# W' = w3·w_out in plain float32 matmuls, from decoded weights that are not split

## Chip, core and metric

One core of one Trainium2 chip runs the kernel. The time is device microseconds (us) of one execution. The kernel shown here took 947.56 us (median of 3 runs, 945.53 to 948.35).

## What is computed

The inputs come as float64, and the kernel decodes each weight to float32 itself. An attention of 4 batches and 8 heads (a pooled one and a local band) gives x of 2304 tokens by 512. Then, cut to what matters:

```python
a = x @ w1                      # 2304 x 1024
b = x @ w2
h = a * b @ w3                  # w3: 1024 x 1024
x = h @ w_out                   # w_out: 1024 x 512
h = x @ w_in                    # 2304 x 2048
out = (h * sigmoid(h)) @ w_out2 # 2304 x 512
```

The kernel multiplies w3 and w_out first, into W' (1024 x 512), so that the two products of the third and fourth line become one, `(a * b) @ W'`. The change is in how W' is made.

## The kernel before

**Weights.** A piece of a weight is 128 x 512 numbers of 8 bytes. `load_w` (L110) issues its DMA on SP's queue into a staging tile `st`; there are four of them in the opening, so up to four pieces are under way. `decode` makes float32 of it: one ScalarE instruction (ACT, L123) takes the high word's magnitude, and four VectorE instructions (DVE, L133, L137, L142, L147) shift and join the bits, in a tile `dec`. The last of the four is the last to read `st`, and frees it for the next load. `parts` then splits the float32 number in two: ACT rounds it to fp32r, the high part (`nc.scalar.copy`, L159), and DVE subtracts to get the low part (L160). A split weight is a tile of two layers, `[P, 2, 1024]`.

**Products.** Matmuls of split operands are made in three passes (`PASSES`): high by high, low by high, high by low. `wprime(i)` (L407) is a quarter of the work on one pair of tiles: two column blocks j, each with three matmuls of 128 x 512 into a PSUM tile `wp`; four quarters use up one w3 tile. In all it issues 192 matmuls from 8 w3 tiles (named `w_w` in the trace; two buffers) and 4 w_out tiles (`w_wA`; four buffers). Finished sums are split into `w_wC` (L421, L422).

**Order.** The opening is laid out by `events`: 36 attention steps (`run_steps`), 32 quarters of `wprime`, and decoding jobs with due slots. The jobs are 8 pieces of w_out, 16 of w3 and the first 8 of w1 and w2 (`w_wB`). The tile scheduler takes that list and fixes one order for each engine; within an engine instructions run strictly in that order. SP's queue too is in order: loads of the attention's q, k and v (`qk`, `vw`, `vr`) stand between the weight loads. The attention's matmuls are plain float32: scores `sd`, `s`; outputs `od`, `ol`; transposes `td`, `tl`. After the opening the a and b products (`ab`, L500), the product with W' (`y`, L533) and the second network (`h`, L670 and `o`, L697) follow; w1 and w2's last 8 pieces are decoded during the first `ab` products.

Of the kernel before, what the change touches and what calls it, by code (L numbers as in the profile page):

```python
# [8 lines left out]
F32 = mybir.dt.float32  # L9
# [5 lines left out]
NB, NHP, S, P = 4, 4, 576, 128  # L15
# [10 lines left out]
PASSES = ((0, 0), (1, 0), (0, 1))  # L26
I32 = mybir.dt.int32
# [5 lines left out]
def tile_model(ctx: ExitStack, tc: tile.TileContext, qk, vw, vr, w12, w3t, wo, wb, out):  # L33
    nc = tc.nc
    wide = wo.dtype != F32
# [20 lines left out]
    def mm_tile(name):  # L56
        return ps.tile([P, 512], F32, tag="mm", name=name, bufs=4)
# [27 lines left out]
    W = {}  # L85
    raw = {}
    homes = [stg]
    dec_homes = [stg, w3pool]
# [15 lines left out]
    def load_w(key, t):  # L104
# [8 lines left out]
            nc.sync.dma_start(st, src)  # L113
        raw[key, t] = (st, home)

    def decode(pair):

        todo = []
        for key, t, where, tag, bufs in pair:
            st, home = raw.pop((key, t))  # L120
            if wide:
                v = dec_homes[t % len(dec_homes)].tile([P, 512], I32, tag="dec", name="dec", bufs=2)
                nc.scalar.activation(v.bitcast(F32), st[:, :, 1].bitcast(F32), AF.Abs)  # L123
                todo.append((v, st))
            else:
                todo.append((st, st))

        def bits():
            if not wide:
                return  # L130
            for v, st in todo:
                f = v.bitcast(F32)
                nc.vector.tensor_scalar(  # L133
                    out=f, in0=f, scalar1=E_LOW, scalar2=E_HIGH, op0=ALU.max, op1=ALU.min
                )
            for v, st in todo:
                nc.vector.tensor_scalar(  # L137
                    out=v, in0=v, scalar1=3, scalar2=0x3FFFFFF8,
                    op0=ALU.logical_shift_left, op1=ALU.bitwise_and,
                )  # L140
            for v, st in todo:
                nc.vector.scalar_tensor_tensor(  # L142
                    out=v, in0=st[:, :, 1], scalar=-0x40000000, in1=v,
                    op0=ALU.bitwise_and, op1=ALU.bitwise_or,
                )
            for v, st in todo:
                nc.vector.scalar_tensor_tensor(  # L147
                    out=v, in0=st[:, :, 0], scalar=29, in1=v,
                    op0=ALU.logical_shift_right, op1=ALU.bitwise_or,
                )  # L150

        def parts():
            for (key, t, where, tag, bufs), (v, st) in zip(pair, todo):
                if t == 0:
                    W[key] = where.tile([P, 2, 1024], F32R, tag=tag, name="w_" + tag, bufs=bufs)
                f = v.bitcast(F32) if wide else v
                hi = W[key][:, 0, t * 512:(t + 1) * 512]
                lo = W[key][:, 1, t * 512:(t + 1) * 512]
                nc.scalar.copy(hi, f)  # L159
                nc.vector.tensor_tensor(out=lo, in0=f, in1=hi.bitcast(F32), op=ALU.subtract)  # L160

        bits()
        parts()

    def key_pieces(key, where, tag, bufs=None):
# [230 lines left out]
    def wprime(i):  # L396
        step, q = divmod(i, 4)
        half, gp = divmod(step, 4)
        k, jj = divmod(q, 2)
        w3v = W["w3", (gp, half)].rearrange("p l (k f) -> p l k f", k=2)  # L400
        wov = W["wo", gp].rearrange("p l (k e) -> p l k e", k=2)
        for j in (2 * jj, 2 * jj + 1):
            if gp == 0 and k == 0:
                wp_ps[j] = mm_tile(f"wp{half}_{j}")
            acc = wp_ps[j]
            for n, (a, b) in enumerate(PASSES):
                nc.tensor.matmul(  # L407
                    acc, lhsT=w3v[:, a, k, j * P:(j + 1) * P], rhs=wov[:, b, k, :],
                    start=(gp == 0 and k == 0 and n == 0),
                    stop=(gp == 3 and k == 1 and n == 2),  # L410
                )
        if q == 3:
            W.pop(("w3", (gp, half)))
        if gp == 3 and k == 1:
            for j in (2 * jj, 2 * jj + 1):
                m = 4 * half + j
                acc = wp_ps[j]
                if m % 2 == 0:
                    WP[m // 2] = wpool.tile([P, 2, 2, 512], F32R, tag="wC", name="w_wC")
                d = WP[m // 2]  # L420
                nc.scalar.copy(d[:, 0, m % 2, :], acc)  # L421
                nc.vector.tensor_tensor(  # L422
                    out=d[:, 1, m % 2, :], in0=acc, in1=d[:, 0, m % 2, :].bitcast(F32),
                    op=ALU.subtract,
                )
# [18 lines left out]
    for n, slot in enumerate((0, 1, 3, 5, 7, 8, 10, 11)):  # L444
        m, t = 4 + n // 2, n % 2
# [10 lines left out]
    def run_plan(slot):  # L456
        while n_jobs[0] < len(jobs) and jobs[n_jobs[0]][0] <= slot:
            pieces = jobs[n_jobs[0]][1]
            n_jobs[0] += 1
            n_done[0] += len(pieces)  # L460
            decode(pieces)
            load_to(n_done[0] + 4)
# [12 lines left out]
    for when, kind, i in sorted(events):  # L475
        if kind == 0:
            run_plan(when)
        elif kind == 1:
            wprime(i)
        else:  # L480
            run_steps(i + 1)
# [135 lines left out]
    def wb_next():  # L617
        n = n_split[0]
        if n >= min(32, 2 * len(wb_home)):
            return  # L620
        where, tag, bufs = wb_home[n // 2]
        wb_load(n + 1)
        decode([(("wb", n // 2), n % 2, where, tag, bufs)])
        n_split[0] += 1
        wb_load(n + 1 + 2 * len(homes))
# [88 lines left out]
    for s in range(16 * NT + LAG):  # L714
        if s < 16 * NT:
            t, f = divmod(s, 16)
# [65 lines left out]
```

## Time and profile before

| What | Value |
|---|---|
| Median of 3 runs | 947.56 us |
| The profiled execution's own time | 947.99 us |
| Its span in the profile | 946.2 us |
| PE busy | 892.4 us (94%) |
| DVE busy | 459.7 us (49%) |
| ACT busy | 317.1 us (34%) |
| Chain that ended last: PE, DVE, DMA, ACT | 73%, 12%, 6%, 4% |

PE is TensorE, PEld its weight loads, POOL is GpSimd. Busy shares are means over the whole run. The kernel has stages with different limits, so the table alone does not say what bounds the stage of the change. PEclk is the granted share of TensorE's clock: 1.00 is 2.4 GHz, 0.50 is 1.2 GHz, and a value between is a mean over time at both.

### The profile page before, as it was taken

Reading aid. Unit: us, or ns where it says so; the run is one execution under the profiler, and the core shown is the slowest. Engines: PE = TensorE matmul, PEld = TensorE weight load, DVE = VectorE, ACT = ScalarE, POOL = GpSimd, SP = SyncE. Lnnn points to the kernel's source line nnn. Section 1 sums busy time; section 2 is a strip of 40 time slices with the busy share of each in tenths; the row PEclk is TensorE's granted clock in tenths of the full one; section 3 lists DMA queues with packets and bytes.
Section 4 is the critical chain, followed back from the end, with each engine's and each line's share of the span. In section 5 each row is a group of like instructions: output and inputs, shape, how many; then the busy total and the mean of one; then the engine's idle time right before and its main releaser. Section 6 shows DMA issues by size and latency. Waiting matters only on the chain.

```text
span 946.2 us, 15978 instructions
## 1 busy us (share of the span) xinstructions
PE 892.4 (94%) x6224; PEld 802.3 (85%) x6224; DVE 459.7 (49%) x997; ACT 317.1 (34%) x966; POOL 258.0 (27%) x269
## 2 busy tenths in 40 slices
PE   5767789999999999999999998999999999999998
PEld 4545578899989999999999897989989989999897
DVE  7888999635453444324637999222221221222221
ACT  6466675443333333334224533211211211111111
POOL 1000014434243333324112154422422423322221
PEclk9787999999999999999999999999999999999999
DMA  8555544221422121121512544200200000000000
GB/s 272 167 179 182 185 132 127 63 76 56 139 78 77 58 72 53 31 68 40 178 65 75 185 139 133 63 6 1 68 1 1 34 1 1 34 1 1 35 1 34
DMA packets 26285, 73.58 MB, mean 78 GB/s; under 512 B 2912, under 2 KB 10080, under 8 KB 26208
## 3 DMA queue, kind: packets, MB, share of 16 engines
q1 hardware_dynamic: 26208, 72.54, 24.3%
q8 instruction: 49, 0.80, 0.4%
q14 instruction: 28, 0.23, 0.1%
HBM read 63.09 MB, written 9.44 MB: 77 GB/s over the span
## 4 chain that ended last, share of the span: by engine, by line
PE 73%; DVE 12%; DMA 6%; ACT 4%; issue 3%; POOL 1%; SPq 0%; DVEq 0%; ACTq 0%; POOLq 0%
PE o L697 19%; PE h L670 19%; PE ab L500 18%; PE y L533 9%; DVE dec L142 3%; DMA st<-wb 3%; DVE dec L147 2%; DMA st<-w3t 2%; PE ol L341 1%; PE s L300 1%; DVE dec L133 1%; DMA st<-w 1%; DVE dec L137 1%; PE tl L325 1%; ACT dec L123 1%
## 5 line engine op out<-in xcount | busy, mean ns | idle before, releaser
L681 POOL TENSOR_TENSOR g<-gf,g 128x384 fp32r<-128x384 f32 x96 | 104.8, 1092 | 275.9 <-DVE g L680 275.9
L678 DVE TENSOR_TENSOR gf<-h,sg 128x384 f32<-128x384 f32 x96 | 53.4, 556 | 258.7 <-ACT sg L676 258.7
L676 ACT ACTIVATE sg<-h 128x384 f32<-128x384 f32 x96 | 47.0, 491 | 290.3 <-PE h L670 290.3
L500 PE MATMUL ab<-x,w_wA 128*128 128x320 f32 (+1 forms) x768 | 112.7, 300 | 0.8 <-DVE w_wA L160 0.8
L500 PE MATMUL ab<-x,w_wB 128*128 128x320 f32 (+1 forms) x768 | 113.2, 300 | 0.0
L533 PE MATMUL y<-c,w_wC 128*128 128x320 f32 (+1 forms) x768 | 111.2, 299 | 0.0
L500 PEld LDWEIGHTS ab<-x,w_wA 128*128 128x128 f32 x768 | 103.2, 188 | 4.4 <-issue 2.0
L500 PEld LDWEIGHTS ab<-x,w_wB 128*128 128x128 f32 x768 | 103.6, 188 | 2.6 <-issue 0.8
L533 PEld LDWEIGHTS y<-c,w_wC 128*128 128x128 f32 x768 | 102.9, 188 | 2.7 <-issue 1.6
L518 POOL TENSOR_TENSOR c<-cf,c 128x320 fp32r<-128x320 f32 (+1 forms) x64 | 54.8, 856 | 140.2 <-DVE c L517 120.5
L407 PE MATMUL wp<-w_wA,w_w 128*128 128x512 f32 x192 | 63.4, 477 | 13.1 <-ACT w_w L159 12.0
L123 ACT ACTIVATE dec<-st 128x512 f32<-128x512 f32 x72 | 48.4, 674 | 69.9 <-DMA st<-wb 30.9
L224 ACT ACTIVATE E<-E,sm 128x70 f32<-128x70 f32 x144 | 49.0, 342 | 49.0 <-DVE sm L220 49.0
L407 PEld LDWEIGHTS wp<-w_wA,w_w 128*128 128x128 f32 x192 | 41.4, 228 | 24.9 <-ACT w_w L159 14.1
L514 DVE TENSOR_TENSOR cf<-ab,af 128x320 f32<-128x320 f32 (+1 forms) x64 | 29.0, 453 | 66.3 <-PE ab L500 60.1
L697 PE MATMUL o<-w_wA,g 128*128 128x512 f32 x216 | 55.7, 401 | 4.2 <-POOL g L681 3.6
L670 PE MATMUL h<-yhl,w_wC 128*128 128x384 f32 x288 | 55.2, 341 | 0.0
L670 PE MATMUL h<-yhl,w_wB 128*128 128x384 f32 x288 | 54.2, 337 | 0.5 <-ACT yo L542 0.5
L670 PE MATMUL h<-yhl,w_wA 128*128 128x384 f32 x288 | 54.4, 337 | 0.0
L697 PE MATMUL o<-w_wB,g 128*128 128x512 f32 x216 | 54.2, 395 | 0.0
L697 PE MATMUL o<-w_wC,g 128*128 128x512 f32 x216 | 54.1, 395 | 0.0
L670 PEld LDWEIGHTS h<-yhl,w_wC 128*128 128x128 f32 x288 | 52.0, 191 | 2.2
(92 smaller groups left out, 1377.6 us busy)
## 6 DMA issues: line engine op xcount, KB each, us to landing
st<-wb SPq DMA_DIRECT2D x32, 512.0 KB, 4.1
qk<-qk SPq DMA_DIRECT2D x16, 579.0 KB, 3.8
st<-w3t SPq DMA_DIRECT2D x16, 512.0 KB, 5.2
st<-w SPq DMA_DIRECT2D x16, 512.0 KB, 4.6
vw<-vw SPq DMA_DIRECT2D x16, 360.0 KB, 3.7
vr<-vr SPq DMA_DIRECT2D x16, 320.0 KB, 3.2
st<-ydram SPq DMA_DIRECT2D x12, 384.0 KB, 3.3
out<-os SPq DMA_DIRECT2D x18, 256.0 KB, 2.1
```

Source lines behind the costliest of these rows:

```text
L123: nc.scalar.activation(v.bitcast(F32), st[:, :, 1].bitcast(F32), AF.Abs)
L224: nc.scalar.activation(E[:, j, :], src[:, j, :], AF.Exp, bias=nb[:, j:j + 1], scale=scale, accum_out=sv[:, j:j + 1],)
L407: nc.tensor.matmul(acc, lhsT=w3v[:, a, k, j * P:(j + 1) * P], rhs=wov[:, b, k, :], start=(gp == 0 and k == 0 and n == 0), stop=(gp == 3 an ...
L500: nc.tensor.matmul(acc[:, :N], lhsT=wv[:, i, w, kk, :], rhs=x[:, j, :], start=(n == 0), stop=(n == 11),)
L514: nc.vector.tensor_tensor(out=cf, in0=acc[:, :N], in1=C.pop("af"), op=ALU.mult)
L518: nc.gpsimd.tensor_tensor(out=c[:, 1], in0=cf, in1=c[:, 0].bitcast(F32), op=ALU.subtract)
L533: nc.tensor.matmul(acc[:, :N], lhsT=WP[kf // 2][:, i, kf % 2, ec * P:(ec + 1) * P], rhs=c[:, j, :], start=(kf == 0 and n == 0), stop=(kf = ...
L670: nc.tensor.matmul(acc[:, :TT], lhsT=w[:, i, kk, :], rhs=y[:, j, kk, :], start=(n == 0), stop=(n == 11),)
L676: nc.scalar.activation(sg, acc[:, :TT], AF.Sigmoid)
L678: nc.vector.tensor_tensor(out=gf, in0=acc[:, :TT], in1=sg, op=ALU.mult)
L681: nc.gpsimd.tensor_tensor(out=g[:, 1], in0=gf, in1=g[:, 0].bitcast(F32), op=ALU.subtract)
L697: nc.tensor.matmul(acc_ps[t][j], lhsT=g[:, a, j * P:(j + 1) * P], rhs=w[:, b, 512:1024], start=(f == 0 and n == 0), stop=(f == 15 and n == 2),
```

## The change

Pieces of w3 and w_out are decoded straight into the tile from which the matmuls read, as float32, and are not split. `whole` gives that place: one `[P, 2, 512]` tile for two pieces of w3, and one `[P, 2, 2, 512]` tile for four pieces of w_out. `wprime` then makes one plain float32 matmul where three fp32r ones stood, 64 in all. w1, w2 and the second network's weights are decoded and split as before.

```diff
+    def whole(key, t, where, tag, bufs):
+        kind, i = key
+        if kind == "w3":
+            if t == 0:
+                W[key] = where.tile([P, 2, 512], I32, tag=tag, name="w_" + tag, bufs=bufs)
+            return W[key][:, t, :]
+        if i % 2 == 0 and t == 0:
+            W["wo2", i // 2] = where.tile([P, 2, 2, 512], I32, tag=tag, name="w_wo", bufs=bufs)
+        W[key] = W["wo2", i // 2][:, i % 2]
+        return W[key][:, t, :]
...
             st, home = raw.pop((key, t))
+            if key[0] in ("wo", "w3"):
+                v = whole(key, t, where, tag, bufs)
...
+            elif wide:
+                v = dec_homes[t % len(dec_homes)].tile([P, 512], I32, tag="dec", name="dec", bufs=2)
             if wide:
-                v = dec_homes[t % len(dec_homes)].tile([P, 512], I32, tag="dec", name="dec", bufs=2)
...
         def parts():
             for (key, t, where, tag, bufs), (v, st) in zip(pair, todo):
+                if key[0] in ("wo", "w3"):
+                    continue
...
-            for n, (a, b) in enumerate(PASSES):
-                nc.tensor.matmul(
-                    acc, lhsT=w3v[:, a, k, j * P:(j + 1) * P], rhs=wov[:, b, k, :],
-                    start=(gp == 0 and k == 0 and n == 0),
-                    stop=(gp == 3 and k == 1 and n == 2),
-                )
+            nc.tensor.matmul(
+                acc, lhsT=w3v[:, k, j * P:(j + 1) * P], rhs=wov[:, k, :],
+                start=(gp == 0 and k == 0), stop=(gp == 3 and k == 1),
+            )
```

The scheduler makes new orders from this. Line numbers of the changed kernel are 18 to 20 higher behind the new function (L123 is L141, L341 is L361, L407 is L426).

On PE, here is the first w3 tile's work in the kernel before, from the third column block of its first half on (`wp` are the W' sums, `w_w_185` the w3 tile, `tl`, `od`, `ol` the attention's):

```order
L407 MATMUL wp_2_326<-w_wA,w_w_185 128x512 x3
L407 MATMUL wp_3_330<-w_wA,w_w_185 128x512 x3
L325 MATMUL tl_0_0_300<-ident,E_0_152 70x128 x2
L325 MATMUL tl_0_2_304<-ident,E_0_152 70x128 x3
L407 MATMUL wp_0_311<-w_wA,w_w_185 128x512
L407 MATMUL wp_1_315<-w_wA,w_w_185 128x512
L285 MATMUL od_319<-EdT_192,vd_205 64x144 x4
```

And the same place in the changed kernel, where the w3 tile is `w_w_172` and the w_out tile `w_wo`:

```order
L426 MATMUL wp_2_297<-w_wo,w_w_172 128x512
L426 MATMUL wp_3_299<-w_wo,w_w_172 128x512
L345 MATMUL tl_0_0_275<-ident,E_0_152 70x128 x2
L345 MATMUL tl_0_2_279<-ident,E_0_152 70x128 x2
L426 MATMUL wp_0_286<-w_wo,w_w_172 128x512
L345 MATMUL tl_0_2_279<-ident,E_0_152 70x128
L305 MATMUL od_290<-EdT_186,vd_199 64x144 x4
```

Each three has become one, at nearly the same places among the attention's matmuls.

On SP's queue, these are the weight loads of the third group (w_out, then w3) and what stands around them, before:

```order
L110 DMA st<-w3t 128x1024 x2
L188 DMA vw_488<-vw 80x1152
L110 DMA st<-wo 128x1024 x2
L110 DMA st<-w3t 128x1024 x2
L181 DMA qk_587<-qk 128x1158
```

And in the changed kernel:

```order
L110 DMA st<-w3t 128x1024 x2
L110 DMA st<-wo 128x1024 x2
L208 DMA vw_427<-vw 80x1152
L110 DMA st<-w3t 128x1024 x2
L201 DMA qk_505<-qk 128x1158
```

The load of `vw` has moved behind the two w_out loads.

On ACT, the changed kernel has this around the decoding of the third w3 tile, `w_w_334` (what an instruction waits for stands in brackets; `DMAHW` is a load's landing):

```order
L256 ACTIVATE E_1_256<-E_1_256,sm 128x70 [waits Activation_49] x3
L141 ACTIVATE w_wo<-st 128x512 [waits DMAHW7_49]
L244 ACTIVATE Ed_356,sm<-sd_349,sm 128x144 [waits DVE_49,PE_49]
L141 ACTIVATE w_w_334<-st 128x512 [waits DMAHW0_49,PE_49]
L244 ACTIVATE Ed_356,sm<-sd_349,sm 128x144 x2
L346 COPY ET_1_371<-tl_1_0_372 70x256 [waits PE_49]
```

Before, a decode wrote `dec` first, and only the split wrote the w3 tile:

```order
L123 ACTIVATE dec<-st 128x512 [waits DMAHW6_49,DVE_49]
L159 CAST w_w_263<-dec 128x512 [waits DVE_49]
L123 ACTIVATE dec<-st 128x512 [waits DMAHW7_49,Activation_49]
L159 CAST w_w_263<-dec 128x512 [waits DVE_49]
L224 ACTIVATE E_1_281,sm<-E_1_281,sm 128x70 [waits DVE_49]
```

The casts are gone from ACT's order, and the first instruction of a decode now waits for PE as well, which must be done with the w3 tile whose buffer it writes.

## Rows read from the trace of the kernel before

**Rows 1.** Busy us (instructions) by stretch: PE, PEld, DVE, ACT, POOL; PEclk; DMA; GB/s.

```profile
0.00:134.50 134.50, 96.20 (x631) 69.94 (x632) 113.68 (x255) 83.90 (x256) 5.46 (x15) 0.86 0.60 191
134.50:175.00 40.50, 36.37 (x326) 32.69 (x325) 40.46 (x83) 23.00 (x77) 15.96 (x16) 1.00 0.33 101
175.00:580.00 405.00, 400.00 (x3488) 376.05 (x3486) 214.88 (x473) 153.40 (x527) 130.33 (x144) 1.00 0.29 89
580.00:946.00 366.00, 359.81 (x1786) 323.58 (x1784) 90.73 (x190) 56.77 (x109) 106.20 (x95) 1.00 0.06 21
```

**Rows 2.** Groups on DVE, 0 to 134.5 us: busy us, mean ns, idle before.

```profile
L160 DVE TENSOR_TENSOR w_w<-dec,w_w 128x512 fp32r<-128x512 f32 x16 | 10.7, 686 | 6.6 <-ACT w_w L159 6.6
...
L160 DVE TENSOR_TENSOR w_wA<-dec,w_wA 128x512 fp32r<-128x512 f32 x8 | 5.4, 682 | 0.0
```

**Rows 3.** Groups on ACT, 0 to 134.5 us, same columns.

```profile
L159 ACT CAST w_w<-dec 128x512 fp32r<-128x512 f32 x16 | 9.4, 611 | 4.9 <-DVE dec L147 4.9
...
L159 ACT CAST w_wA<-dec 128x512 fp32r<-128x512 f32 x8 | 4.9, 613 | 0.4 <-DVE dec L147 0.4
```

**Rows 4.** Chain that ended last, in the opening: start us, length us, what.

```profile
12.99 0.59 DVE w_wA L160
...
28.86 4.69 DMA st<-w3t
...
42.94 0.27 ACT w_w L159
...
61.77 3.78 PE wp L407 x8
...
91.64 0.60 DVE w_w L160
...
104.69 1.71 PE wp L407 x4
...
110.32 4.73 DMA st<-w
...
117.28 0.52 ACT w_w L159
...
117.84 2.08 PE wp L407 x4
```

**Rows 5.** Groups on PE, whole run: plain float32 scores and transposes.

```profile
L300 PE MATMUL s<-qk 64*64 64x70 f32 x576 | 27.8, 238 | 6.1 <-DVE E L310 3.1 <-ACT Ed L224 3.0
L325 PE MATMUL tl<-ident,E 128*70 128x128 f32 x144 | 25.2, 287 | 8.6 <-DVE ods L290 3.0 <-ACT EdT L275 2.4 <-ACT E L236 1.6
```

**Rows 6.** The chain where PE works without a pause, at PEclk 1.00.

```profile
186.75 0.88 PE sd L251 x12
...
201.75 0.55 PE tl L325 x5
...
589.80 2.10 PE o L697 x9
```

**Rows 7.** SP's queue in order of time, 36 to 52 us.

```profile
42.31 0.33 SPq L188 DMA_DIRECT2D vw<-vw  x1
42.74 0.84 SPq L110 DMA_DIRECT2D st<-wo  x2
```

**Rows 8.** DVE and ACT in order of time, 28 to 50 us.

```profile
33.62 0.68 ACT L123 ACTIVATE dec<-st 128x512 f32<-128x512 f32 x1 [1.65 <-DMA st<-w3t]
...
37.27 1.28 DVE L147 SCALAR_TENSOR_TENSOR dec<-st,dec 128x512 int32<-128x512 int32 x2
...
48.42 0.69 DVE L160 TENSOR_TENSOR w_w<-dec,w_w 128x512 fp32r<-128x512 f32 x1 [3.79 <-ACT w_w L159]
```

**Rows 9.** PE's W' matmuls in order of time: the ends of the first two w3 tiles.

```profile
22.82 2.36 PE L407 MATMUL wp<-w_wA,w_w 128*128 128x512 f32 x9
...
42.20 5.46 PE L407 MATMUL wp<-w_wA,w_w 128*128 128x512 f32 x22
```

**Rows 10.** The W' matmuls, 0 to 134.5 us: busy us, mean ns, idle before.

```profile
L407 PE MATMUL wp<-w_wA,w_w 128*128 128x512 f32 x192 | 63.4, 477 | 13.1 <-ACT w_w L159 12.0 <-DVE w_wC L422 0.8 <-DVE dec L133 0.3
```

More of the change, by code (lines that the diff above doesn't have):

```diff
@@ L120, in decode @@
             st, home = raw.pop((key, t))
+            if key[0] in ("wo", "w3"):
+                v = whole(key, t, where, tag, bufs)
+                if not wide:
+                    nc.vector.tensor_copy(v.bitcast(F32), st)
+                    continue
+            elif wide:
+                v = dec_homes[t % len(dec_homes)].tile([P, 512], I32, tag="dec", name="dec", bufs=2)
             if wide:
-                v = dec_homes[t % len(dec_homes)].tile([P, 512], I32, tag="dec", name="dec", bufs=2)
                 nc.scalar.activation(v.bitcast(F32), st[:, :, 1].bitcast(F32), AF.Abs)
@@ L153, in parts @@
             for (key, t, where, tag, bufs), (v, st) in zip(pair, todo):
+                if key[0] in ("wo", "w3"):
+                    continue
                 if t == 0:
@@ L399, in wprime @@
         k, jj = divmod(q, 2)
-        w3v = W["w3", (gp, half)].rearrange("p l (k f) -> p l k f", k=2)
-        wov = W["wo", gp].rearrange("p l (k e) -> p l k e", k=2)
+        w3v = W["w3", (gp, half)].bitcast(F32)
+        wov = W["wo", gp].bitcast(F32)
         for j in (2 * jj, 2 * jj + 1):
```

## Prediction

> **What bounds the kernel now.** I first read the busy times by stretch [rows 1]. From 175 us on PE is busy 400.0 of 405 and 359.8 of 366 us: whatever comes earlier moves the end by the same amount, as long as it only shifts this part. From 134.5 to 175 us DVE is busy 40.46 of 40.50 us, with work that the change leaves alone (the decoding of the last eight pieces), so this stretch is also shifted as a whole. The change therefore acts in the opening, 0 to 134.5 us, and pays what it takes from the opening's end. There no engine is full: DVE 113.7 us (85%), PE 96.2 us (72%, at a mean clock of 0.86), ACT 83.9 us.
>
> Since no engine fills the opening, busy time alone doesn't price the change. The second view is the chain that ended last [rows 4]: it runs mostly along DVE, and five times (the first at 28.86 us, the last at 110.32 us) leaves it for a weight load of some 5 us and ACT's start of a decode. The third, order of time on SP, DVE and ACT [rows 7, 8], shows why DVE stands idle at one place.
>
> **What is removed.** 24 pieces (16 of w3, 8 of w_out) lose the cast and the subtraction. On DVE that is 10.7 + 5.4 = 16.1 us [rows 2], on ACT 9.4 + 4.9 = 14.3 us [rows 3]. These are upper bounds of what each engine can give. What counts first is what of them stands on the chain [rows 4]: nine pieces of `w_w` or `w_wA` L160, the first of 0.59 us at 12.99 and the last of 0.60 us at 91.64, sum 5.59 us; and five pieces of L159, from 42.94 to 117.28 us, sum 2.84 us. The first of these, 0.27 us, lies in a stall that I count below, which leaves 2.57. Removed: 8.2 us. The rest of the 16.1 us lies beside loads, ACT and PE in the opening, and I count it at nothing; if that cover went with it, 16.1 us is the gain (first rival).
>
> **What is put in its place on PE.** 192 fp32r matmuls become 64 plain ones. Where PE works without pause, nine fp32r matmuls of 512 columns take 2.10 us [rows 6], 0.233 us each, so three take 0.700 us and all 44.8 us at the full clock. A plain 128x512 matmul is not in this trace; three kinds of plain float32 rows bound it. A plain matmul leaves two records: the program issues 18 score matmuls for each of 16 units, 288, and the trace has 576, while the 9 transposes per unit leave 144, one each [rows 5]. Five transposes of 128 columns take 0.55 us [rows 6], 0.110 us a record; four times the columns and two records make 0.880 us for a plain 128x512 matmul. Twelve records of `sd` with 144 columns take 0.88 us. They use quarters of the array, and if they ran one by one, 512 columns would cost 2 x 0.0733 x 512/144 = 0.52 us; if always two ran side by side, 1.04 us. I take the transposes' 0.880 us, since these fill the rows of the array as the new matmuls do; the ends are 0.52 and 1.04. That is 1.257 times the three that go (0.745 to 1.490), and 56.3 us in all: PE gets 11.5 us more work at the full clock.
>
> Three pieces of W' matmuls stand on the chain, 3.78 + 1.71 + 2.08 = 7.57 us [rows 4]. Times 1.257 they cost 1.9 us more (from 1.9 less to 3.7 more). The other W' matmuls are covered by PE's 38.3 us of idle time; that cover gone is the last rival.
>
> A rule to weigh against this price: the Trainium skill, FP8 and Floating Point Precision, TensorE Precision Notes, says that a true float32 product takes four passes through the array, where a reduced one reads the number once. Four passes at the 0.233 us of a row would be 0.93 us a matmul, and the term on the chain 2.5 us instead of 1.9; no row here shows a 512-column one, and the rule makes the change dearer by 0.6 us, not wrong.
>
> **What is moved.** In SP's order the load of `vw` stood ahead of two w_out loads, and now stands behind them. Before, it waited for PE and was issued at 42.31 us; the w_out loads came behind it at 42.74 us [rows 7], although the last readers of the first staging tile had started at 37.27 us and the two were done by 38.55 [rows 8]. DVE then stood idle for 3.79 us, since the cast that it needed was queued on ACT behind the start of a decode that waited for these loads. With the loads issued some 5 us earlier and the cast gone, I take the whole 3.8 us off. The next two loads, of w3, are now the first behind `vw`. They wait for the same step of PE, whose W' matmuls ahead of it are fewer but longer; I take no stall for them, because DVE has the two w_out pieces to decode meanwhile, four instructions each. If they do stall, the 3.8 us are lost again.
>
> **What is added: a wait.** The first ACT instruction of a w3 decode now writes the w3 tile, of which there are two, so it waits until PE has finished with the tile before last. Behind it in ACT's order stand softmax steps (`Ed`) and copies of `ET` from PSUM; DVE's four instructions of that piece wait for it, and PE for those. In the trace of before the first W' tile's matmuls were done at 25.2 us [rows 9], and the third w3 tile's first load was taken up at 33.62 us [rows 8]; the second tile's were done by 47.7 us at the latest [rows 9]. Loads come some 4 us earlier and PE is about 1.4 us later per tile (24 x 0.233 x 0.257), so the first of these waits is covered by the load's landing. I count all six at nothing; if each cost its 1.4 us, that would be 8.6 us. Less than nothing it can't be, since it only delays.
>
> **The sum,** against the profiled execution's 947.99 us (0.43 above the median of 947.56): -5.6 (DVE on the chain) -2.6 (ACT on the chain) +1.9 (PE on the chain) -3.8 (the stall behind `vw`) = -10.1, so **937.9 us**.
>
> **Rivals.**
> 1. *DVE was the true bound of the opening.* With every subtraction gone the end moves by all 16.1 us: 931.9 us. For it speaks that DVE is 85% busy in the opening and full behind it; against it, that the chain leaves DVE for loads five times. It needs the loads to keep ahead of a DVE that is faster by 0.68 us a piece.
> 2. *The stall only changes its place.* The w3 loads, now right behind `vw`, are late in the w_out loads' stead. Then only the chain's own pieces go: 947.99 - 6.3 = 941.7 us.
> 3. *The new wait is paid.* All six w3 tiles wait for PE, 8.6 us: 946.5 us, no change that can be told.
> 4. *PE becomes the bound of the opening* (slower). PE is idle for 38.3 us there, of which 12.0 us is W' waiting for the casts that go [rows 10]; 26.3 us of other waits would stay. PE's busy 96.2 us grow by 11.5/0.86 = 13.4 us at the mean clock, and by 23 us at half the clock: 135.9 to 145.5 us instead of 134.5, so 1.4 to 11 us slower, in the middle 954 us. It decides once the added work is over the 12.0 us that go. For it speaks that the attention's matmuls are queued among the W' ones, so that each longer one delays a softmax; against it, that a part of the 26.3 us is waiting for DVE, which now has less to do.
>
> On the last one the clock matters. PEclk is 0.86 in the opening and 1.00 in the stretches where PE is busier [rows 1]. The Trainium skill, TensorE: Matmul & The Clock Gate, Part 1, says that the slow clock is the default and that activity releases it. By that, a denser PE gets the full clock for longer and the added work nears 11.5 us, below the 12.0 that go. The trace's two stretches agree. I give the rival 12% and not more.
>
> **Chances and range.** Forecast (about 934 to 941) 42%, rival 1 20%, rival 2 17%, rival 3 9%, rival 4 12%. A measurement of this kernel tells a change from none at about 0.3%, 2.8 us: the forecast and rivals 1 and 2 are faster (79%), rival 3 the same (9%), rival 4 slower (12%). The range takes in rival 1 with a little room below and rival 3 above: 930.5 to 947.0. It leaves out rival 4 and some 4% at the low end. The bounds of the plain matmul's price (+1.8 and -3.8 us around the sum) lie inside.
>
> **What would show it.** In the profile after: no L159 and L160 for w3 and w_out, DVE's busy time less by about 16 us, ACT's by about 14. Plain W' matmuls in 128 records, following each other at about 0.44 us where PE doesn't pause (0.26 or 0.52 at the bounds). The first `ab` matmul about 10 us earlier than before, and all from there on shifted by as much, with the same lengths. The w_out loads of the third group issued close to the freeing of their tiles. It would be wrong if the start of a w3 decode on ACT waits for PE by microseconds (rival 3); if PE is busy nearly all of the opening (rival 4); if the w3 loads behind `vw` leave DVE idle (rival 2); or if DVE's idle time in the opening is as it was, so that the full 16 us come off (rival 1).

## The result, and the profile after

The changed kernel takes 930.39 us (median of 4 runs, 928.24 to 932.21), the kernel before 946.54 us (4 runs). The ratio is 0.983, 95% interval 0.9808 to 0.9852: about 16 us faster, a little under the low end of the range (930.5 to 947.0) and well over the 10.1 us of the sum. Rival 1, 931.9 us, has the number that came. One of the twelve executions of e2 below took 1711.85 us, and its ratio leaves that one out.

The busy times by stretch of the changed kernel (columns as in [rows 1]); the opening ends 16 us earlier, so the stretches start 16 us earlier too:

```profile
0.00:118.50 118.50, 95.66 (x578) 51.08 (x579) 99.92 (x236) 72.44 (x236) 5.47 (x15) 0.97 0.69 217
118.50:159.00 40.50, 36.69 (x335) 33.12 (x336) 39.28 (x82) 22.87 (x81) 17.65 (x18) 1.00 0.33 101
...
159.00:564.00 405.00, 399.45 (x3470) 375.31 (x3468) 213.41 (x468) 151.69 (x519) 128.81 (x142) 1.00 0.29 89
564.00:930.00 366.00, 359.99 (x1787) 323.72 (x1785) 91.53 (x190) 56.69 (x109) 106.09 (x95) 1.00 0.07 21
```

All behind the opening is as it was, within 1.8 us an engine and stretch, and from 159 us on PE is busy nearly all the time (399.45 of 405 us, then 359.99 of 366). In the opening PE is busy for nearly the same time in a shorter stretch, and its clock is at 0.97 instead of 0.86.

To compare the openings at the same point of the program, I take the stretch up to DVE's first instruction on an `ab` product (`cf`). First the kernel before, then the changed one:

```profile
0.00:139.70 139.70, 101.40 (x666) 74.98 (x667) 118.84 (x266) 87.34 (x268) 6.97 (x16) 0.87 0.58 186
```

```profile
0.00:121.00 121.00, 98.16 (x595) 53.58 (x596) 102.42 (x242) 74.38 (x243) 5.75 (x16) 0.97 0.68 215
```

DVE has 24 instructions fewer (266, 242) and 16.4 us less to do, and reaches the point 18.7 us earlier. Its idle time is 20.9 us before and 18.6 us after: the work taken off came off the time in full, with some idle time besides, and waits for loads, ACT and PE did not fill the hole.

Of those 18.7 us some were lost again at one place behind the opening, in this execution. PE's order of time there, in the changed kernel:

```profile
247.25 0.49 PE L288 MATMUL td<-ident,Ed 128*72 128x128 f32 x3
250.04 0.52 PE L288 MATMUL td<-ident,Ed 128*72 128x128 f32 x3 [2.30 <-DVE xf L372]
250.32 2.90 PE L518 MATMUL ab<-x,w_wA 128*128 128x320 f32 x12
```

And in the kernel before:

```profile
265.27 0.49 PE L268 MATMUL td<-ident,Ed 128*72 128x128 f32 x3
267.25 0.52 PE L268 MATMUL td<-ident,Ed 128*72 128x128 f32 x3 [1.49 <-DVE xf L352]
267.53 2.02 PE L500 MATMUL ab<-x,w_wA 128*128 128x320 f32 x12
```

Up to here the changed kernel is 18.0 us ahead (265.27 to 247.25). PE then waits 2.30 us instead of 1.49, and the twelve matmuls behind take 2.90 us instead of 2.02. What is left at the end is 946.2 - 930.4 = 15.8 us of span.

### The profile page after: what moved, and what is told of

Its sections match the earlier page's. It is cut to its first block, busy times and chain, and to the rows that moved or that the text cites. A ratio compares the mean times of both kernels' runs of the same rounds, so it can differ in the third digit from the quotient of the medians.

```text
span 930.4 us, 15783 instructions
## 1 busy us (share of the span) xinstructions
PE 891.8 (96%) x6160; PEld 783.2 (84%) x6160; DVE 444.2 (48%) x973; ACT 303.7 (33%) x942; POOL 258.0 (28%) x269
## 4 chain that ended last, share of the span: by engine, by line
PE 72%; DVE 13%; DMA 7%; issue 3%; ACT 3%; POOL 1%; SPq 0%; DVEq 0%; ACTq 0%; POOLq 0%
PE o L715 20%; PE h L688 19%; PE ab L518 16%; PE y L551 8%; DMA st<-wb 3%; DMA st<-w3t 2%; DVE dec L160 2%; DVE dec L165 2%; PE wp L426 2%; PE s L320 2%; PE ol L361 2%; PE tl L345 1%; DMA st<-w 1%; DVE dec L155 1%; DVE dec L151 1%
## 5 line engine op out<-in xcount | busy, mean ns | idle before, releaser
L426 PE MATMUL wp<-w_wo,w_w 128*128 128x512 f32 x128 | 64.6, 637 | 4.9 <-DVE w_w L165 4.9
L688 PEld LDWEIGHTS h<-yhl,w_wB 128*128 128x128 f32 x288 | 50.9, 188 | 2.5 <-ACT yo L560 0.6
L688 PEld LDWEIGHTS h<-yhl,w_wA 128*128 128x128 f32 x288 | 51.2, 188 | 2.1
```

Of the source, the lines that this page charges most:

```text
L426: nc.tensor.matmul(acc, lhsT=w3v[:, k, j * P:(j + 1) * P], rhs=wov[:, k, :], start=(gp == 0 and k == 0), stop=(gp == 3 and k == 1),)
L688: nc.tensor.matmul(acc[:, :TT], lhsT=w[:, i, kk, :], rhs=y[:, j, kk, :], start=(n == 0), stop=(n == 11),)
```

## Experiments

Each time is a median; the ratio is to the kernel before on the same chip, from all the runs and not from the medians, with its 95% interval. The medians of before lie between 945.6 and 947.0 us. Between two experiments I compare medians, and read differences under some 3 us as none.

| Run | us | ratio | interval |
|---|---|---|---|
| Changed kernel | 930.39 | 0.983 | 0.9808 to 0.9852 |
| e1: before, no subtractions | 929.25 | 0.981 | 0.9772 to 0.9847 |
| e2: before, no casts | 943.09 | 0.9973 | 0.995 to 0.9996 |
| e3: changed, subtractions back | 940.51 | 0.9935 | 0.9912 to 0.9959 |
| e4: before, one `vw` load from GpSimd | 943.71 | 0.998 | 0.9959 to 1.0001 |
| e5: changed, less on PE | 929.6 | 0.9827 | 0.98 to 0.9854 |
| e6: changed, more on PE | 941.26 | 0.9945 | 0.9923 to 0.9967 |
| e7: changed, `w_wB` subtracted on GpSimd | 925.61 | 0.9793 | 0.9767 to 0.9818 |
| e8: changed, clamp on GpSimd | 933.26 | 0.9871 | 0.9844 to 0.9897 |
| e9: changed, casts back | 929.0 | 0.9819 | 0.979 to 0.9847 |
| e10: changed, both back | 940.25 | 0.9949 | 0.9932 to 0.9966 |
| e11: changed, three kinds on GpSimd | 928.51 | 0.9819 | 0.9791 to 0.9847 |
| e12: changed, four kinds on GpSimd | 929.87 | 0.9845 | 0.9815 to 0.9876 |

**e1, the subtractions alone.**

```diff
-                nc.vector.tensor_tensor(out=lo, in0=f, in1=hi.bitcast(F32), op=ALU.subtract)
+                if key[0] not in ("wo", "w3"):
+                    nc.vector.tensor_tensor(out=lo, in0=f, in1=hi.bitcast(F32), op=ALU.subtract)
...
-                    acc, lhsT=w3v[:, a, k, j * P:(j + 1) * P], rhs=wov[:, b, k, :],
+                    acc, lhsT=w3v[:, 0, k, j * P:(j + 1) * P], rhs=wov[:, 0, k, :],
```

> The kernel before without the 24 subtractions of w3 and w_out on VectorE (about 16.1 us there); casts, 192 fp32r matmuls and load sizes stay, and all three passes read the high layer, so the low parts are left out. Theory A (the opening is bound by VectorE's work, whichever piece of it goes): about 16 us faster, 930 us. Theory B (my prediction's: only what stands on the chain, 5.6 us, and the 3.8 us stall behind the load of vw, which stands behind the w_out loads here too): 937 us. Theory C (the gain over the chain comes from the plain matmuls, which keep TensorE's clock up): without them only the chain's pieces, 940 us, and a granted clock in the opening as before.

It is as fast as the changed kernel, with all casts and all 192 fp32r matmuls in place (six runs, 923.62 to 932.02 us). Up to DVE's first `cf`:

```profile
0.00:124.20 124.20, 99.22 (x660) 74.74 (x661) 102.77 (x242) 86.25 (x267) 6.73 (x16) 0.88 0.67 209
```

DVE has the changed kernel's 242 instructions, ACT still has its casts, and PE's clock is at 0.88, hardly over the 0.87 before. Theory A's time came and B's 937 us did not; C, by which the gain needs the plain matmuls to keep the clock up, falls. But the edit did one thing more: SP's order moved, and the load of `vw` stands behind the two w_out loads, as in the changed kernel:

```profile
32.84 1.99 SPq L110 DMA_DIRECT2D st<-wo  x2
36.46 0.33 SPq L189 DMA_DIRECT2D vw<-vw  x1
```

So what the subtractions give and what the moved load gives are not apart in e1.

**e2, the casts alone.** ACT's casts of w3 and w_out go, DVE subtracts (a constant column), and the matmuls read the layer that it writes.

```diff
+                if key[0] in ("wo", "w3"):
+                    nc.vector.tensor_tensor(out=lo, in0=f, in1=ident[:, 0:1].to_broadcast([P, 512]), op=ALU.subtract)
+                    continue
...
-                    acc, lhsT=w3v[:, a, k, j * P:(j + 1) * P], rhs=wov[:, b, k, :],
+                    acc, lhsT=w3v[:, 1, k, j * P:(j + 1) * P], rhs=wov[:, 1, k, :],
```

> The kernel before without the 24 casts of w3 and w_out on ScalarE (about 14.3 us there); a subtraction on VectorE for each piece stays, and all three passes read the layer that it writes. Theory A: VectorE has the same work, so nothing, 946 us, or the little that its waits for casts cost. Theory B: 2.6 us of the chain and the 3.8 us stall, 940 us. Theory C: 944 us.

943.09 us: the 14.3 us of ACT's work are worth some 3 us, nearest to C's figure and between A's and B's. The load of `vw` has moved behind the w_out loads in this kernel as well, so the casts may be worth less. From e2 to e1 (subtractions out, casts back), with that order in both, it is 13.8 us.

**e3, the subtractions put back,** as a subtraction of a column of zeros (`zero`).

```diff
                 if key[0] in ("wo", "w3"):
+                    f = v.bitcast(F32)
+                    nc.vector.tensor_tensor(out=v.bitcast(F32), in0=f, in1=zero.to_broadcast([P, 512]), op=ALU.subtract)
                     continue
```

> The changed kernel with one subtraction of zero on VectorE for each of the 24 pieces, in place, after the decode: some 0.68 us each, 16.4 us in all; plain matmuls, no casts. Theory A: nearly all of it comes back, 944 to 947 us. Theory B: only the 5.6 us that stood on the chain, 936 us. Theory C: the clock stays up with the plain matmuls, so 936 us or less.

940.51 us: 10 us come back, not 16 as A said, nor 6 as B said. This is the cleanest price of the subtractions, since all else is the changed kernel and `vw` stays behind the w_out loads. The matmuls wait for these subtractions too, so it is the price of the work and of that wait together. Up to the first `cf`:

```profile
0.00:131.90 131.90, 102.69 (x602) 55.98 (x603) 117.40 (x266) 75.78 (x246) 7.05 (x17) 0.94 0.63 198
```

DVE has its 266 instructions and 117.4 us of work again, 15 us more, but it is idle for 14.5 us, less than in either kernel: a part of the work that was put back falls into time in which DVE had been idle.

**e4, the stall behind `vw`.**

```diff
-        nc.sync.dma_start(t, vw[u // 4, u % 4])
+        (nc.gpsimd if u == 1 else nc.sync).dma_start(t, vw[u // 4, u % 4])
```

> The kernel before with the second load of vw issued from GpSimd's queue, which is idle then; the order on VectorE is the same to the row. The w_out loads behind it on SP no longer wait for TensorE. Theory B: VectorE's stall of 3.8 us goes and the end comes as much earlier, 943 us. Theory A: the work is the same and VectorE must make up for a later wait, so between nothing and 3.8 us. If the stall only changes its place (rival 2 of the prediction): 946 us.

The w_out loads are issued 4 us earlier, at 38.60 us instead of 42.74. In order of time on SP, and on DVE where it had waited 3.79 us [rows 8]:

```profile
38.60 0.92 SPq L110 DMA_DIRECT2D st<-wo  x2
```

```profile
45.47 0.69 DVE L160 TENSOR_TENSOR w_w<-dec,w_w 128x512 fp32r<-128x512 f32 x1 [0.27 <-ACT w_w L159]
```

That stall is gone, but among DVE's waits (total, times, longest) up to 134 us there is now one of 4.5 us for a cast:

```profile
DVE w_w L160 <- ACT w_w L159: 5.0, 3, 4.5
```

It comes at a pair of subtractions that had waited for 1.11 us in the kernel before, and the cast is late because ACT had waited for a W' sum of PE. In order of time, DVE and then ACT:

```profile
73.23 1.30 DVE L160 TENSOR_TENSOR w_w<-dec,w_w 128x512 fp32r<-128x512 f32 x2 [4.45 <-ACT w_w L159]
```

```profile
69.88 0.59 ACT L421 CAST w_wC<-wp 128x512 fp32r<-128x512 f32 x1 [4.40 <-PE wp L407]
```

PE's matmuls ahead of it ran at another clock. The same eight records in the kernel before, then in e4, and 5 us of that place in the same order (PEclk 0.88 and 0.50):

```profile
68.59 2.13 PE L407 MATMUL wp<-w_wA,w_w 128*128 128x512 f32 x8
```

```profile
67.34 3.75 PE L407 MATMUL wp<-w_wA,w_w 128*128 128x512 f32 x8
```

```profile
65.00:70.00 5.00, 5.00 (x50) 3.66 (x49) 3.76 (x12) 2.06 (x9) 0.00 (x0) 0.88 0.11 43
```

```profile
65.00:70.00 5.00, 5.00 (x20) 3.43 (x20) 3.78 (x9) 0.60 (x5) 0.00 (x0) 0.50 0.27 66
```

So the stall came back 25 us later: at 73.23 us e4 is no longer ahead of the kernel before (72.87), and PE at its low clock took a part of it. That is the kind of thing rival 2 names, though not at its place, the w3 loads behind `vw`. The time is at most a little lower: the interval, 0.9959 to 1.0001, takes in no gain and one of 3.9 us.

**e5 and e6, less and more work on PE.** In e5, 48 of the 64 matmuls have 128 columns instead of 512; in e6, 32 of the 64 are made twice.

```diff
+            N = 512 if (gp == 0 and k == 0) or (gp == 3 and k == 1) else 128
             nc.tensor.matmul(
-                acc, lhsT=w3v[:, k, j * P:(j + 1) * P], rhs=wov[:, k, :],
+                acc[:, :N], lhsT=w3v[:, k, j * P:(j + 1) * P], rhs=wov[:, k, :N],
```

> The changed kernel with 48 of the 64 plain matmuls made over 128 columns in place of 512 (three quarters of their columns of W' left out): TensorE has some 32 us less to do in the opening, VectorE and ScalarE the same. Theory A (VectorE's work bounds the opening, TensorE's is covered): 930 us as the changed kernel, at most 2 us less. Theory B (the chain that ended last prices an edit): W' matmuls stand there with about 17 us in the changed kernel, of which a half would go: 921 us. Theory C (a busier TensorE keeps its clock and so shortens the opening): the clock falls again and the time rises, 932 us or more.

```diff
-            nc.tensor.matmul(
-                acc, lhsT=w3v[:, k, j * P:(j + 1) * P], rhs=wov[:, k, :],
-                start=(gp == 0 and k == 0), stop=(gp == 3 and k == 1),
-            )
+            for n in range(2 - k):
+                nc.tensor.matmul(
+                    acc, lhsT=w3v[:, k, j * P:(j + 1) * P], rhs=wov[:, k, :],
+                    start=(gp == 0 and k == 0 and n == 0), stop=(gp == 3 and k == 1),
+                )
```

> The changed kernel with every second plain matmul made twice (W' is then not the product): 32 more of 0.88 us, 28 us more on TensorE in the opening. TensorE is idle there for 22.9 us of 118.5. Theory A: what exceeds the cover is paid and the rest isn't, 5 to 10 us, 935 to 940 us. Theory B: the share of the 17 us on the chain, half as much again, 939 us. Rival 4 of the prediction (TensorE is the bound already): all of it, 958 us.

Up to the first `cf`, e5 and then e6:

```profile
0.00:121.40 121.40, 79.98 (x596) 58.98 (x597) 103.80 (x242) 75.02 (x243) 6.75 (x16) 0.76 0.69 214
```

```profile
0.00:131.10 131.10, 120.94 (x652) 62.76 (x653) 113.93 (x258) 77.52 (x249) 8.59 (x16) 1.00 0.67 210
```

In e5 some 32 us of matmuls at the full clock are gone (an estimate: 48 times three quarters of 0.88 us). PE's busy time falls by only 18 us, as its clock is down at 0.76. Nothing is gained (929.6 us): PE is covered.

In e6, 28 us more (32 times 0.88, an estimate), 11 us are paid. Its first `cf` is not the same point of the program: in its order three pieces of `w_wA` are decoded ahead of it, so DVE has 258 instructions there and 11.5 us more to do. The stretch from 60 us to the start of the last W' matmul can be compared, in e6 and then in the changed kernel:

```profile
60.00:122.80 62.80, 62.45 (x310) 29.96 (x308) 57.19 (x128) 39.42 (x127) 2.81 (x2) 1.00 0.60 192
```

```profile
60.00:110.40 50.40, 43.99 (x240) 21.61 (x240) 43.67 (x104) 32.77 (x108) 0.00 (x0) 0.93 0.62 196
```

PE is busy for 62.45 of 62.8 us at the full clock, and the last W' matmul starts 12.4 us later. Beyond its idle time PE does become the bound, as rival 4 had it, only not with the change's own 11.5 us.

**e9 and e10, the casts put back,** without and with the subtractions of e3:

```diff
                 if key[0] in ("wo", "w3"):
+                    nc.scalar.copy(v.bitcast(F32), v.bitcast(F32))
                     continue
```

```diff
+                    f = v.bitcast(F32)
+                    nc.scalar.copy(f, f)
+                    nc.vector.tensor_tensor(out=f, in0=f, in1=zero.to_broadcast([P, 512]), op=ALU.subtract)
```

> The changed kernel with one ScalarE copy of each of the 24 pieces back, in place, ahead of the plain matmuls (0.61 us each, 14.7 us in all). Theory A (VectorE's work sets the opening's end): nothing or the 2 to 3 us that the casts gave when they alone were left out, 930 to 933 us. Theory B (ScalarE's pieces on the chain): 933 us.

> The changed kernel with both the copy on ScalarE and the subtraction of zero on VectorE back for each of the 24 pieces; the plain matmuls wait for both. Only the kind of matmul and the place of the decode still differ from the kernel before. If casts and subtractions together are all of the change's gain: 946 us. If the plain matmuls, that wait for one tile and need no low part, give something of their own: 941 to 944 us.

Now the eight cases are nearly complete (us):

| Matmuls | both | no casts | no subtractions | neither |
|---|---|---|---|---|
| three fp32r | 946.54 | 943.09 | 929.25 | not run |
| one plain | 940.25 | 940.51 | 929.0 | 930.39 |

The column without subtractions is the fast one, whatever else is there. With plain matmuls the casts are worth nothing (940.25 and 940.51; 929.0 and 930.39). And once the subtractions are gone, the plain matmuls add nothing (929.25 and 929.0). While they are there, the plain form is some 5 to 6 us faster (946.54 and 940.25; by e10's ratio 4.8 us), so subtractions and matmul kind are not independent. One thing goes with that difference: DVE's wait for casts, 6.6 us in the kernel before [rows 2], is nearly gone in e10 (up to 120 us), though its subtractions also follow a copy on ACT:

```profile
DVE w_w L177 <- ACT w_w L176: 0.3, 1, 0.3
```

That wait is not all of it: e2 has no casts to wait for, and it gained only some 3 us. In e10 a decode no longer waits for a `dec` tile, SP's order has `vw` behind the w_out loads (alone worth 3.9 us at most, e4), the matmuls are fewer, and PE's clock up to the first `cf` is higher (0.92, and 0.94 in e3, against 0.87 before and 0.85 in e2); which of these gives the 5 to 6 us was not told apart. That stays open.

**e7, e8, e11, e12: more off VectorE.** If DVE's work is what counts, GpSimd, idle in the opening, can take more of it. e7 gives it the eight subtractions of `w_wB`:

```diff
-                nc.vector.tensor_tensor(out=lo, in0=f, in1=hi.bitcast(F32), op=ALU.subtract)
+                eng = nc.gpsimd if opening[0] else nc.vector
+                eng.tensor_tensor(out=lo, in0=f, in1=hi.bitcast(F32), op=ALU.subtract)
```

> The changed kernel with the eight subtractions of w_wB in the opening made on GpSimd, which is idle there, in place of VectorE (8 of 0.69 us, 5.5 us). Theory A: the opening ends about 5 us earlier, 925 us, less what GpSimd's work slows on VectorE. Theory B: four pieces of it stand on the chain, the rest is covered, so 925 us as well; if the longer GpSimd instructions hold up a later load or product, 930 us.

925.61 us, the lowest median here: its five runs (924.96 to 927.15) all lie below the four of the changed kernel. The medians are 4.8 us apart; by the ratios it is 3.5 us, and the intervals overlap a little. Both theories had forecast 925 us, so the time does not decide between them, and the trace does not bear A out. Up to the first `cf`:

```profile
0.00:117.90 117.90, 100.31 (x603) 55.02 (x604) 104.25 (x236) 74.72 (x246) 18.56 (x24) 0.96 0.71 221
```

DVE has six instructions fewer than in the changed kernel (eight subtractions gone, two others ahead of this point), but 104.25 us of busy time instead of 102.42; what fell is its idle time, from 18.6 to 13.7 us. Other DVE instructions took longer here, also small ones. One of them, in e7 and then in the changed kernel:

```profile
L241 DVE TENSOR_SCALAR sm<-md 128x3 f32<-128x3 f32 x5 | 2.5, 491 | 0.0
```

```profile
L240 DVE TENSOR_SCALAR sm<-md 128x3 f32<-128x3 f32 x5 | 0.8, 162 | 0.0
```

e8 gives GpSimd the clamp, the first of DVE's four steps, of all 32 pieces:

```diff
-                nc.vector.tensor_scalar(
+                (nc.gpsimd if opening[0] else nc.vector).tensor_scalar(
                     out=f, in0=f, scalar1=E_LOW, scalar2=E_HIGH, op0=ALU.max, op1=ALU.min
```

> The changed kernel with the first of VectorE's four steps (the clamp, 0.42 us) of all 32 pieces of the opening made on GpSimd: 13 us off VectorE. GpSimd's step comes between ScalarE's and VectorE's, so each piece takes longer to decode. Theory A with loads well ahead: about 13 us faster, 918 us. If the loop from a freed staging tile through load, ScalarE, GpSimd and VectorE is by then as long as the work (four pieces in 11 to 16 us), little or nothing of it: 926 to 932 us.

933.26 us, nothing of the 13 us. GpSimd's and DVE's groups up to 120 us:

```profile
L151 POOL TENSOR_SCALAR w_w<-w_w 128x512 f32<-128x512 f32 x16 | 32.0, 2007 | 20.1 <-ACT w_w L141 20.1
```

```profile
L160 DVE SCALAR_TENSOR_TENSOR w_w<-st,w_w 128x512 int32<-128x512 int32 x16 | 11.9, 757 | 0.0
...
L155 DVE TENSOR_SCALAR w_w<-w_w 128x512 int32<-128x512 int32 x16 | 8.6, 542 | 5.1 <-POOL w_w L151 5.0
```

A clamp takes GpSimd 2.0 us where DVE took 0.42, DVE waits for it, and DVE's own steps grow: 757 and 542 ns, against these of the changed kernel up to 121 us:

```profile
L160 DVE SCALAR_TENSOR_TENSOR w_w<-st,w_w 128x512 int32<-128x512 int32 x16 | 10.7, 683 | 0.0
...
L151 DVE TENSOR_SCALAR w_w<-w_w 128x512 f32<-128x512 f32 x16 | 6.4, 419 | 0.8 <-ACT w_w L141 0.8
L155 DVE TENSOR_SCALAR w_w<-w_w 128x512 int32<-128x512 int32 x16 | 6.3, 418 | 0.0
```

e11 adds to e7 the additions of `vr` and the subtractions of x in the opening; e12 adds to that the subtractions of `w_wA` behind it. The first cut is e11 against e7, the second e12 against e11; `wb` are weights of the second network.

```diff
...
-        side().tensor_tensor(out=t, in0=r[:, :, 0, :], in1=r[:, :, 1, :], op=ALU.add)
+        nc.gpsimd.tensor_tensor(out=t, in0=r[:, :, 0, :], in1=r[:, :, 1, :], op=ALU.add)
...
-            side().tensor_tensor(
+            nc.gpsimd.tensor_tensor(
                 out=x[:, 1], in0=xf, in1=x[:, 0].bitcast(F32), op=ALU.subtract
```

```diff
-                eng = nc.gpsimd if opening[0] else nc.vector
+                eng = nc.vector if key[0] == 'wb' else nc.gpsimd
```

> The changed kernel with three kinds of VectorE's work in the opening on GpSimd: w_wB's subtractions (as in the run that took 925.6 us), the two additions of vr, and the subtractions of x; about 7 us more off VectorE. Theory A: 920 us; if GpSimd's slower instructions on the attention's way, or VectorE slowed beside it, take that back: 925 us or more.

> The same with the subtractions of w1 and w2's last eight pieces (w_wA, during the first products, where VectorE is busy nearly all of 40 us) on GpSimd too. Theory A carried to that stretch: some 5 us less than the run with three kinds, 915 us; but GpSimd makes the products' low parts there, so it can also hold these up: 920 to 925 us.

928.51 and 929.87 us: neither is faster than e7, nor clear of the changed kernel's 930.39. In e11 the subtractions of x take GpSimd over 2 us each, and DVE, with 19 instructions fewer than in the changed kernel, is busy for longer up to the first `cf` (105.48 us):

```profile
L384 POOL TENSOR_TENSOR x<-xf,x 128x320 fp32r<-128x320 f32 x4 | 8.9, 2232 | 8.9 <-ACT x L383 8.9
```

```profile
0.00:118.70 118.70, 96.26 (x585) 53.16 (x586) 105.48 (x223) 73.99 (x242) 44.18 (x39) 0.98 0.70 223
```

In neither e7 nor e11 did moving work to GpSimd make DVE's busy time less, so these runs do not show what less work on DVE is worth. How much of e11 is DVE's longer instructions and how much is waiting for GpSimd was not told apart.

## Why the prediction was wrong

**The step that failed** is this: "The rest of the 16.1 us lies beside loads, ACT and PE in the opening, and I count it at nothing". Only 5.6 of DVE's 16.1 us were priced. In the changed kernel the 24 subtractions are worth 10 us (e3), and e1, without them and with `vw` moved, is 17 us faster than the kernel before with every cast and fp32r matmul in place. Whatever form the matmuls have, the fast kernels are those without the subtractions.

Rival 1, with 20%, named the sign that came (DVE's idle time hardly changed) and nearly the time. Its mechanism holds in part only: a DVE that is the true bound would have paid 16 us for the subtractions put back in e3, and it paid 10. That its number fits the whole change is in part luck: by e3 and e10 some 10 of the 16 us are the subtractions', and the other 5 to 6 go with the plain form and the orders that it has.

**How the chain misled.** The chain showed nine pieces of subtractions, and ran along ACT ahead of most loads. But a load is issued when DVE has freed its staging tile. SP's waits up to 134.5 us, before (total, times, longest), and DVE in order of time at one load:

```profile
SPq L110 <- DVE dec L147: 68.2, 28, 9.7
```

```profile
54.54 0.68 DVE L147 SCALAR_TENSOR_TENSOR dec<-st,dec 128x512 int32<-128x512 int32 x1
```

The chain has this around the load that follows:

```profile
54.78 0.50 ACT w_wA L159
55.28 5.19 DMA st<-w3t
```

The piece before the load is a cast on ACT, though the last reader of the staging tile, on DVE, ended at 55.22 us (54.54 + 0.68), just before, and the cast does not read that tile. In the changed kernel SP's waits for DVE's last readers sum to 72.8 us, again 28 times. So loads wait for DVE, and DVE, through ACT, for loads; in such a loop instructions of DVE count that one reading of the chain passes by. That this loop is the reason is argued from these rows, not shown by a run, and e3 shows that not every microsecond of DVE counts in full.

**ACT, -2.6 us.** With plain matmuls the casts are worth nothing that can be told (e9, e10). With fp32r they were some 3 us, with `vw` moved too (e2).

**PE, +1.9 us.** The price of a plain matmul was right. Eight records in the chain of the changed kernel take 3.63 us and four 1.72 us; at two records a matmul that is 0.86 to 0.91 us, and 0.880 was forecast:

```profile
94.27 1.72 PE wp L426 x4
95.99 0.62 PE ol L361 x16
96.61 3.63 PE wp L426 x8
```

But on the way to the end it costs nothing: e5 takes more than all of it away and gains nothing. The Trainium skill (FP8 and Floating Point Precision, TensorE Precision Notes) gives a true float32 product four passes; at 0.233 us each that is an estimate of 0.93 us. The measured 0.86 to 0.91 us is near it and a little less; the trace has two records a matmul and does not show passes.

**The stall, -3.8 us.** The place was read rightly, and SP's order did what was expected: in the changed kernel the loads are issued at 35.39 us, ahead of `vw`:

```profile
35.39 1.85 SPq L110 DMA_DIRECT2D st<-wo  x2
37.30 0.42 SPq L208 DMA_DIRECT2D vw<-vw  x1
```

What it is worth stays open: in e4's trace the stall comes back 25 us later, while its time leaves room for all of the 3.8 us or for none.

**The new wait, counted at nothing.** Right: no start of a w3 decode waits for PE in the changed kernel's list of ACT's waits; they wait for loads.

```profile
ACT w_w L141 <- DMA st<-w3t: 9.9, 7, 3.5
```

**Rival 4.** PE's idle time covered the added work, and the clock rose from 0.86 to 0.97, in the direction that the Trainium skill's rule (TensorE: Matmul & The Clock Gate, Part 1: activity releases the slow clock) gives. The rise is not needed for the gain: e1 is as fast at 0.88. Whether the changed kernel, with more on PE, would be as fast at the old clock was not run.

## What to carry to other kernels

Where an engine is 85% busy and feeds a loop of loads and buffers, price its removed work in full as one case of equal weight, and don't price only what stands on the chain: here 5.6 us stood on it and at least 10 were paid. At a wait for several semaphores the chain may name the wrong releaser, so look at what frees the buffer. A single stall that is removed can come back at a later wait (e4). Work that is moved to a neighbouring engine is not work removed: beside GpSimd DVE's busy time did not fall (e7, e11).

To see which part of a change pays, run its parts alone, from before and from after. Here the two directions gave 17 and 10 us for the same subtractions, so the parts do not add up; and the matmuls that the change speaks of were covered.

## What the runs showed of the hardware

- A plain float32 matmul of 128x512 leaves two records, about 0.43 to 0.45 us apart, 0.86 to 0.91 us together, against 0.700 us for three fp32r ones.
- One wait of 2.30 us on PE was followed by twelve matmuls in 2.90 us that took 2.02 us behind a wait of 1.49 us. The row of that stretch, 250 to 262 us of the changed kernel, has PEclk 0.86; the one before has 1.00. In the kernel before, the clock stayed at 1.00 there (256 to 280 us):

```profile
238.00:250.00 12.00, 9.73 (x93) 8.92 (x90) 7.16 (x21) 4.79 (x21) 2.77 (x4) 1.00 0.30 90
250.00:262.00 12.00, 11.96 (x86) 11.07 (x87) 5.56 (x13) 4.05 (x17) 4.41 (x6) 0.86 0.24 80
```

- A clamp of 128x512 float32 took GpSimd 2.0 us and DVE 0.42 us, and in that kernel DVE's shift and join steps of the same tiles took 542 and 757 ns instead of 418 and 683 (e8).
- With eight subtractions on GpSimd, DVE was busy for 104.25 us in 236 instructions, against 102.42 in 242 without; a 128x3 instruction of DVE took 491 ns on average instead of 162 (e7).
- Eight records of fp32r W' matmuls took 2.13 us where PEclk was 0.88 (kernel before), and 3.75 us where it was 0.50 (e4).
